# Turning the first softmax's weights by their layout (fp32 where strided, fp32r where contiguous) under a new order of all steps

## The chip, the cores and the metric

The kernel runs on one core of a Trainium2 chip. The metric is the device time of one execution in microseconds (us). A core has a matrix engine (TensorE, PE in the profile; PEld is its weight load), a vector engine (VectorE, DVE), a scalar engine (ScalarE, ACT), GpSimd (POOL) and a sync engine (SyncE, SP) that issues most of the DMA transfers. Each engine works through its own instructions in the order in which the program lists them and waits for the others through semaphores.

## The reference: what is computed

Two attentions through 32 "packing" queries per head, and then a feed-forward block with a gate from a convolution over the sequence:

```python
p_packed = sm_attn(p, k, v)                 # 8 batches x 8 heads: 32 queries over 576 keys, depth 64
out      = sm_attn(q, p_packed, p_packed)   # 576 queries over those 32
x        = out as [8, 576, 512]
h        = relu(x @ w_in)                   # w_in 512 x 1024
conv     = sum over k of conv_w[k] * h shifted by k - 1 along the sequence
y        = (h * sigmoid(conv)) @ w_out      # w_out 1024 x 512
```

`sm_attn` is scale, softmax (maximum taken off, exponential, division by the sum) and the product with the values. The two weight matrices and `conv_w` arrive as 64-bit floats and are rounded to fp32 on the chip.

## The kernel before, in words

The 64 heads form 16 groups `g` of four heads, so that four times 32 packing queries fill 128 partitions. For each group the kernel loads k, q and v; turns k and q so that the depth lies on the partitions (for the first four groups on TensorE, `half_transpose`, copied out by VectorE or ScalarE; later on VectorE); and runs `attention(g)`: scores of the packing queries with k (L752), maximum on VectorE, exponential on ScalarE (L890) into `a1_sb`, five turns of 128x128 on TensorE (L902), a copy to `a1T`, the product with v (L910), a copy `pb` scaled by the sums, one turn (L933) and its copy `ppT`, the scores with q (L752 again), the second softmax on VectorE, GpSimd and ScalarE, and its result split into a high and a low part in fp32r (`a2hi`, `a2lo`).

The five turns L902 are what the edit touches. They turn the exponentials, 128 queries by 576 keys, in pieces of 128 keys. For the first six groups (`g < APART`) v lies in SBUF with four neighbouring keys on one partition, so the first four turns each read every fourth column of `a1`; the fifth reads 128 neighbouring columns. For the other ten groups all five read neighbouring columns. Before, all five went through `a1_bits`, a view of the same memory as fp32r.

The rest is matrix work per batch `b`: `packed_weight` multiplies the packed values by w_in (L1107) and takes the low part by a matmul with minus the identity (L1135); `ffn1` makes 128 channels of the hidden layer from three fp32r products (L1196; L1170 for the first three channels' blocks of batch 0, which are cut in three steps); ScalarE and VectorE do relu, convolution and gate; `ffn2` multiplies by w_out (L1323 in plain fp32 for the first three tiles of 128 rows, L1376 in three fp32r products later, L1282 for the last tile). The weights of w_in and w_out are rounded by ScalarE (L463, L525: about a microsecond each), VectorE and GpSimd.

The order of everything is fixed ahead. The text `ORDER` names, two letters for a step, which of 268 streams (one per load, per attention, per block of channels and so on) goes next, and each engine gets its instructions in that order. Class `Flow` walks through it with a duration for every step, so as to decide one thing: where TensorE would wait in the first part, it puts matmuls on zeros, `warm` (L306), in the gap, as many as it thinks fit. `ON_DVE` and `ON_POOL` say which copies go to VectorE instead of ScalarE and which additions to GpSimd instead of VectorE. The search that finds `ORDER` is not in the kernel.

Of the kernel before, what the change touches and what calls it, by code (L numbers as in the profile page):

```python
# [18 lines left out]


ORDER = (
    "007f3603076y34023636036y340504050a040506050a70057001343a066z05056z350c34050e36340534050c3b0h0c053b0d0505340c7672"
    "3b0h7209360c050b050505080d713c36050j3b0b0c0c710c0c0j0c05050j0l3d3q053q0g770c0j3q0c0o0k0c3d3q3e0c0i0j3d0o0i0c0c73"
    "3d73740c3s740c3f3q3t3g3q3q0c0c3f780c3t3s3s0f3q3h3f3s0m0n3t3t0k3f793h3u3s0q3t3i3r0j3r0q3t3h0s0q3r3s0r3u3t0j3r3u3u"
    "0r370j0j3s0q0j0q3t0j0q3k3u0q0p3t3u3s0z3s0p753j3h0q3v0q7a753j3u3w0q3v3r3w3j0j3j400j3m0q5y370q3w3u3r0q3v0v405z3r3u"
    "3v603w3r5z5y3x3l7b603l0j3v0q3x3l373v3o403l0j0x0q3x400j0t3w3w3v0q0j0j0q0x5z5y0q123y0x3n0j3y3w0j3y3x3n3y3x60600x7c"
    "3n3y3z0x3z3z5y0j3n1441143p0q410x163x3z0u0q5z413x0y3p60605y0q7d143y3p190y15423z1d5z5z101e3y3j3l421142433z413p0w42"
    "43433z420x425y4444443l4342435z433n1445455y0x3j144515433n46605y441y0x456046464438440x4561451b46446046140x1b14465z"
    "0x471b3p45605y474846476113141g3p494847486149485z491761141b1b49485y1k484747614949486147496161616118141i0x4a141i62"
    "611i621c4b1b62621462621c1j140x630x380x4a1i62621b1b3862141i1b0x624a1i0x1j631a1z0x5z1n1r1b0x62141p626414141p636363"  # L30
    "141f1b0x634b63631b141i4b14631l141i631b4c1b1p4c641b4c1u631q4d1p4d4e1p1i644c1b1h4c4e4d4c1i1q1w1p644d651w1b1m1w644c"
    "4d4e1i251s4d1b4f1i1p4e4d4e4e646364641i641p211w644e654f4g1b1i4f1o1b1i1x4h4f4g641t6565644h1i1i1b4h651w4g4k1p4h4f23"
    "4g4k1i1p1x231w1p4f66651w6565234h4g4f4h4h1w1w4k1i4g6523651i234i6565661i4i1p4i1v284i4j66664j4g4i4j4i2a4l1p1w231w2a"
    "662a4m4i4n4j4j1p4j661p664m664j66664o1w4n4m666724672a244m1p6861391p671p4n1p23674n674o2k23674l2a6767674m4l4m204m4o"
    "4n4p4o232c2b4n66674p4n4q671w262a68391w222f232b4q394p4o4u4q274q4o2j4o234q2a692h2h694q2m1w684u1p4q4p6868681w1p4r4p"
    "4r1w2h68684u682d68682i4s4p2h4s294r4s2a691w6969692a4p692h234t4t2e68694t4s4r69694r2o1w4s4v4t6a6a2o2a692q2h1w6a2i4s"
    "4r6a2x2o4t4t4r6a6a4s4t236a2h2o6b2a236a6b1w2p236a6a69232h676a4w2o2a4x232t4w6b2h2a4w4y4v6c2p6b6b232l2g4w4w6b6b6b4y"
    "234w6b4x4w4z6b4x2v4z4y2z6b4y2a544v6c232h4x2o2v6d4y4z6c4x4x2v6c6a6c4z6c4z4x2h6c6c234y6c542v2h6c6d6c2h504y6b2a6d6e"
    "506d6d506d2h2a6d4z6d306d2r6e2w6c4z2n6d502w6d512v546f506e5051506e2o526e51516f2o516e6d6e53526e512h532o6e2a522a526e"
    "2y532v32556e2h2a2h2o51522a6f2a6f52322h322v556f6f6f2o536e5356522o6f6f6f2h53565757536f6g58562v6g2o562h6g6g6g575856"  # L40
    "576h576g6h566g562o6g586g6g58322o596g6h2o586h5755596h2s6i6g6h575a6h593258332v59585a5a6h6h59596i5a6h5b6j596h5a5a5b"
    "5c2o5c6i6i6j6i5b5a5d6i6i2o6i6h6i2h6i5d5c2u5b5e5c2v6i5f5b326j6j5b5d6j6j6j2o5e6f5d6j6j5c5d5d5c6i5b5e2o5d6j335f5c32"
    "2v2o6k6k5g2v5f5h5g2v5g6j326k6l5i6k5h6k5i5g5h2v326k6k6k5h5h5h316k5i5h5j6k6k5g6l325j5i6k5j325o325j5j5j5i6l6l6l6l6l"
    "6l322v6l6m5j5o6m6l6l5i5g325k5k6j6n6m6m5o6m2v6m6m5g5k5i6m6m5l5l6m2v5m322v6n2v5k6m5k322v5l6n325k6n5k5m6n6m5m5l6n6o"
    "5n5m5m6o326n5n6n5n5n6n6l6n6n2v5l5l5p325n5n6o5m5l326o6n6o5n6o6o5m6p6o326o5p6o5q5q5r5s5r5p6o5q6p6p6p6p6p5q5r5q5s6p"
    "5q5s6q6p5q6p6p5t6q5s6p5t5s5r6q6q5t6r5s6o5t6q5r6q6q5t5s5r5t6q6q5u6r6q5t5r5u6s5u6q5v5w6r6r5u5v5u5u6r5u6r5w5v6s5w6r"
    "5v5w5x6r6p5x5v6r5w5x6r6s5w6s5v6r6s6s6s5x5x5x5w5v6s5x6s6t6s6t6t6u6r6t6t6s6t6t6t6u6t6t6u6u6s6v6v6t6u6u6u6u6u6u6w6v"
    "6v6v6t6v6u6v6v6w6v6v6q6w6u6w6w6w6w6v6w6w6w6x6x6x6x6v6x6x6x6x6x6x6w7e7e6x7e6w7e7e7e7e6x7e7e7e"
)


# [171 lines left out]
def tile_packed_attention_conv_gate(  # L223
# [32 lines left out]
    ON_DVE = {"gh510", "hi0", "hi1", "hi12", "kT00", "kT05", "kT25", "kT30", "qT00", "relu34", "relu76", "tap00", "tap01", "tap21", "tap40", "tap41", "tap42", "tap44", "tap46", "tap53", "tap56", "tap57", "tap60", "tap61", "tap64", "tap65", "tap67", "tap70", "tap72", "tap73", "tap74", "tap75", "tap77", "x140", "x180", "x230", "x270", "x280", "x310", "x340", "x90"}
    ON_POOL = {"add00", "add01", "add10", "add41", "add51", "add61", "add70", "add71", "lo0", "lo10", "lo11", "lo7", "mul10", "mul12", "mul14", "mul2", "mul3", "mul4", "mul5", "mul6", "mul7", "mul9", "sub10", "sub11", "sub15", "sub2", "sub3", "sub4", "sub5", "sub7", "sub8", "sub9", "xl100", "xl110", "xl280", "xl30", "xl320", "xl330", "xl350", "xl50", "xl60", "xl70", "xl80"}
# [1208 lines left out]
```

## Time and profile before

| | |
|---|---|
| median of three runs | 392.18 us (392.03 to 392.35) |
| profiled execution: its own time | 392.02 us |
| its span, first to last instruction | 390.2 us |
| TensorE busy | 384.5 us, 99% of the span |
| VectorE, ScalarE, GpSimd busy | 332.1, 245.0, 73.8 us |
| matmuls on zeros (L306) | 16 |

The profiled execution's time is 1.8 us above its span. A busy interval of TensorE runs from an instruction's start to its modelled end, and neighbours overlap, so 99% busy doesn't mean that it never waited: waits that are shorter than an instruction's way through the array don't show. The distance from one start to the next start tells more.

### The profile page before, as it was taken

The page shows a single profiled execution, that of the slowest core. Times are in us where ns is not written, and L with a number is a line of the kernel's source. Part 1 is how long each engine was busy: PE and PEld are TensorE (multiplying, and loading weights), DVE is VectorE, ACT ScalarE, POOL GpSimd, SP SyncE. Part 2 cuts the span into 40 slices and gives each one's busy share as a digit, 9 for nine tenths or more (in the row PEclk, how much of TensorE's full clock was granted, in tenths as well). Part 3 has the DMA queues.
Part 4 walks back from the last instruction along what each step waited for, and adds up shares of the span by engine and source line. Part 5 has one row for each costly group of instructions (what it writes and reads, how often), then busy time and mean ns, then how long its engine had stood idle before and what let it go on. Part 6 is the DMA issues. An engine that isn't in the chain of part 4 may idle for free.

```text
span 390.2 us, 8180 instructions
## 1 busy us (share of the span) xinstructions
PE 384.5 (99%) x3299; PEld 308.0 (79%) x3299; DVE 332.1 (85%) x495; ACT 245.0 (63%) x403; POOL 73.8 (19%) x58
## 2 busy tenths in 40 slices
...
GB/s 278 372 391 275 198 311 146 203 141 192 93 185 146 179 18 182 198 139 152 116 103 135 29 87 89 0 29 55 29 2 54 55 28 29 27 0 29 81 54 56
DMA packets 157542, 47.62 MB, mean 122 GB/s; under 512 B 145460, under 2 KB 148788, under 8 KB 157504
## 3 DMA queue, kind: packets, MB, share of 16 engines
...
q8 instruction: 26, 0.43, 0.5%
q14 instruction: 12, 0.10, 0.1%
...
## 4 chain that ended last, share of the span: by engine, by line
PE 88%; ACT 4%; DMA 3%; DVE 2%; issue 1%; SPq 1%; ACTq 0%
PE fo L1376 42%; PE big L1196 24%; PE sm L1376 4%; PE big L1323 4%; PE big L752 4%; PE big L1107 3%; DMA k<-in_k_dram 2%; PE sm L910 2%; PE fo L1323 2%; PE big L902 1%; DMA hgt<-in_k_dram 1%; PE fo L1282 1%; PE sm L1282 1%; ACT tmp L463 1%; ACT tmp L525 1%
## 5 line engine op out<-in xcount | busy, mean ns | idle before, releaser
L1376 PE MATMUL fo<-wo_hi,xhi 128*128 128x512 f32 x232 | 93.3, 402 | 0.0
L1376 PE MATMUL fo<-wo_hi,xlo 128*128 128x512 f32 x232 | 90.8, 391 | 0.0
L1376 PE MATMUL fo<-wo_lo,xhi 128*128 128x512 f32 x232 | 90.5, 390 | 0.0
L1213 ACT ACTIVATE hbuf<-big 128x576 f32<-128x576 f32 x62 | 40.2, 656 | 45.7 <-PE big L1196 45.4
L1245 DVE SCALAR_TENSOR_TENSOR hgt<-hbuf,cw,hgt 128x576 f32<-128x576 f32 x64 | 53.4, 842 | 4.2 <-ACT hgt L1243 3.9
L1196 PE MATMUL big<-a2hi,ghi 128*128 128x288 f32 x244 | 55.3, 308 | 0.0
L1253 ACT ACTIVATE hgt<-hgt 128x576 f32<-128x576 f32 x64 | 43.3, 685 | 17.7 <-DVE hgt L1249 17.4
L1376 PEld LDWEIGHTS fo<-wo_hi,xhi 128*128 128x128 f32 x232 | 43.5, 188 | 11.3 <-issue 1.4
L1196 PE MATMUL big<-a2hi,glo 128*128 128x288 f32 x244 | 52.3, 295 | 0.0
L1196 PE MATMUL big<-a2lo,ghi 128*128 128x288 f32 x244 | 52.3, 295 | 0.0
L1249 DVE SCALAR_TENSOR_TENSOR hgt<-hbuf,cw,hgt 128x576 f32<-128x576 f32 x64 | 51.1, 810 | 0.5
L1376 PEld LDWEIGHTS fo<-wo_hi,xlo 128*128 128x128 f32 x232 | 43.6, 188 | 9.6
L1255 DVE SCALAR_TENSOR_TENSOR hgt<-hgt,hbuf 128x576 f32<-128x576 f32 x64 | 47.4, 752 | 3.4 <-ACT hgt L1253 2.8
L1376 PEld LDWEIGHTS fo<-wo_lo,xhi 128*128 128x128 f32 x232 | 43.6, 188 | 7.1
L1196 PEld LDWEIGHTS big<-a2hi,ghi 128*128 128x128 f32 x244 | 41.2, 189 | 6.2 <-issue 2.4
L352 POOL TENSOR_TENSOR xlo<-hgt,xhi 128x1024 fp32r<-128x1024 f32 x11 | 28.0, 2544 | 93.9 <-ACT xhi L359 38.2
L1391 ACT COPY o<-fo 128x512 f32<-128x512 f32 x30 | 17.5, 584 | 35.5 <-PE fo L1376 27.7
L1196 PEld LDWEIGHTS big<-a2lo,ghi 128*128 128x128 f32 x244 | 39.2, 189 | 0.0
L1196 PEld LDWEIGHTS big<-a2hi,glo 128*128 128x128 f32 x244 | 39.1, 188 | 0.0
L1243 ACT ACTIVATE hgt<-hbuf,cw 128x576 f32<-128x576 f32 x42 | 32.5, 778 | 2.9 <-DVE hbuf L1211 2.4
L352 POOL TENSOR_TENSOR s<-s,mx 128x576 f32<-128x576 f32 x10 | 14.3, 1433 | 100.6 <-DVE hgt L1249 58.4
L359 ACT CAST xhi<-hgt 128x1024 fp32r<-128x1024 f32 (+1 forms) x28 | 26.6, 952 | 9.2 <-PE fo L1376 4.0
...
## 6 DMA issues: line engine op xcount, KB each, us to landing
...
```

Of the source, the lines that this page charges most:

```text
L352: added = nc.gpsimd.tensor_tensor(**kw)
L359: nc.scalar.copy(out=out, in_=in_)
L1196: nc.tensor.matmul(out=t[:, hf, :SH], lhsT=w[:, gg, js], rhs=x[:, hf * SH : (hf + 1) * SH], start=n == 0, stop=n == (1 if b in F1F else 3) ...
L1213: nc.scalar.activation(out=inner, in_=t[:, :, :SH], func=AF.Relu, scale=0.5)
L1243: nc.scalar.activation(out=d, in_=h[:, 1 : S + 1], func=AF.Copy, scale=cw[:, NJ + j : NJ + j + 1])
L1245: nc.vector.scalar_tensor_tensor(out=d, in0=h[:, 0:S], scalar=cw[:, j : j + 1], in1=d, op0=ALU.mult, op1=ALU.add)
L1249: nc.vector.scalar_tensor_tensor(out=d, in0=h[:, 2 : S + 2], scalar=cw[:, 2 * NJ + j : 2 * NJ + j + 1], in1=d, op0=ALU.mult, op1=ALU.add)
L1253: nc.scalar.activation(out=d, in_=d, func=AF.Tanh)
L1255: nc.vector.scalar_tensor_tensor(out=d, in0=d, scalar=1.0, in1=h[:, 1 : S + 1], op0=ALU.add, op1=ALU.mult)
L1323: nc.tensor.matmul(out=t, lhsT=src[:, c, :], rhs=w32[c // 2][:, c % 2, :], start=c == 0, stop=c == NJ - 1)
L1376: nc.tensor.matmul(out=t, lhsT=x[:, c, :], rhs=w[:, c % 2, :], start=c + i == 0, stop=c == NJ - 1 and i == 2)
L1391: nc.scalar.copy(out=o, in_=t)
```

## The change

The turns of the strided pieces (four of five in groups 0 to 5) read `a1` as fp32 with the fp32 identity; the contiguous pieces (one of five there, all five from group 6 on) keep the fp32r view. The planner's durations are changed for these turns, for several loads and for the queue of transfers, and `ORDER`, `ON_DVE` and `ON_POOL` are those of a new search.

```diff
 ORDER = (
-    "007f3603076y34023636036y340504050a040506050a70057001343a066z05056z350c34050e36340534050c3b0h0c053b0d0505340c7672"
+    "3600367f07036y03366y340502010a053470050a0570050435063a04346z066z0534340e090c05050c36083b053b34053c0c76050d050c0h"
...
+    AHEAD = 2600
...
+            if step.issue:
+                at = max(at, self.data - self.AHEAD)
...
-    ON_POOL = {"add00", "add01", "add10", ...
+    ON_POOL = {"add01", "add10", ...
...
-        yield Step("SP", 3450, take=["kq"], sets=[(name, g)], parts=4, late=700, issue=830)
+        yield Step("SP", 3700 + 150 * (name == "q"), take=["kq"], sets=[(name, g)], parts=4, late=150, issue=810)
...
-        yield Step("PE", 544, take=["big", "a1T"], give=["a1"], cols=1280)
+        yield Step("PE", 525 if g < APART else 450, take=["big", "a1T"], give=["a1"], cols=1152 if g < APART else 640)
         t = big().rearrange("r f s -> r (f s)")
         for si in range(SV + 1):
-            if si == SV:
-                rows = a1_bits[:, S - 128 :]
-            elif g < APART:
-                rows = a1_bits[:, : 128 * SV].rearrange("c (r s) -> c s r", s=SV)[:, si, :]
+            if si < SV and g < APART:
+                rows = a1[:, : 128 * SV].rearrange("c (r s) -> c s r", s=SV)[:, si, :]
+                nc.tensor.transpose(out=t[:, si * 128 : (si + 1) * 128], in_=rows, identity=ident)
             else:
-                rows = a1_bits[:, 128 * si : 128 * si + 128]
-            nc.tensor.transpose(out=t[:, si * 128 : (si + 1) * 128].bitcast(F32R), in_=rows, identity=ident_r)
+                lo = min(128 * si, S - 128)
+                out = t[:, si * 128 : (si + 1) * 128].bitcast(F32R)
+                nc.tensor.transpose(out=out, in_=a1_bits[:, lo : lo + 128], identity=ident_r)
```

The added lines move the line numbers by three to four: L306 becomes L309, L463 L466, L728 L731, L752 L755, L910 L914, L933 L937, L1107 L1111, L1170 L1174, L1196 L1200; L902 becomes L902 (fp32) and L906 (fp32r).

How the order moves work, at three places. First TensorE in the first 20 us, from the product with v of group 0 to the turns of the keys of group 2 (`k`); `hgt_79` holds keys and queries of the first two groups, `stage` packing queries. Before:

```order
L910 MATMUL sm<-v_92,a1T 32x64 x20
L752 MATMUL big<-kT,pT 32x288 x8
L933 MATMUL sm<-ident,pb 128x128
L306 MATMUL idle<-zeros 128x512 x2
L539 MATMUL sm<-ident,cw_raw 128x24
L752 MATMUL big<-qT,ppT 32x288 x8
L728 MATMUL big<-ident,k 128x128 x5
L902 MATMUL big<-ident_r,a_bits 128x128 x5
L728 MATMUL big<-ident,k 128x128 x4
```

Of the change:

```order
L914 MATMUL sm<-v_92,a1T 32x64 x20
L755 MATMUL big<-kT,pT 32x288 x8
L937 MATMUL sm<-ident,pb 128x128
L309 MATMUL idle<-zeros 128x512 x5
L542 MATMUL sm<-ident,cw_raw 128x24
L755 MATMUL big<-qT,ppT 32x288 x8
L902 MATMUL big<-ident,a_sb 128x128 x4
L906 MATMUL big<-ident_r,a_bits 128x128
L731 MATMUL big<-ident,k 128x128 x9
L731 MATMUL big<-ident,hgt_79 128x128 x5
```

The turns of group 1's exponentials now stand ahead of the turns of the keys of group 2, and five matmuls on zeros instead of two fill the time up to the scores with q of group 0.

Second, ScalarE in the same stretch, from the copy `pb` of group 0 on (`tmp<-hgt_80` is the rounding of the first quarter of w_in, `ppT` what the scores with q wait for, `a_sb` the exponentials of group 1). Before:

```order
L923 ACTIVATE pb<-sm,rs 128x128
L359 COPY qT<-big 128x512
L545 ACTIVATE minus<-ident 128x128
L936 COPY ppT<-sm 128x128
L463 ACTIVATE tmp<-hgt_80 128x1024
L890 ACTIVATE a_sb,sm_266<-big,nm 128x576
```

Of the change:

```order
L927 ACTIVATE pb<-sm,rs 128x128
L466 ACTIVATE tmp<-hgt_80 128x1024
L940 COPY ppT<-sm 128x128
L894 ACTIVATE a_sb,sm_269<-big,nm 128x576
L528 ACTIVATE tmp<-hgt_80 128x1024
L362 COPY a1T<-big 128x640
```

The rounding of w_in now stands ahead of the copy `ppT`; it stood behind it.

Third, TensorE ahead of the first matmuls of `ffn1` (L1170, L1174): from the first product with w_in to them. Before:

```order
L1107 MATMUL big<-w_in_sb,ppT 32x256 x8
L902 MATMUL big<-ident_r,a_bits 128x128 x5
L306 MATMUL idle<-zeros 128x512 x2
L1135 MATMUL big<-ghi,minus 128x256 x2
L728 MATMUL big<-ident,k 128x128 x5
L306 MATMUL idle<-zeros 128x512 x2
L728 MATMUL big<-ident,q 128x128 x9
L728 MATMUL big<-ident,k 128x128 x4
L1170 MATMUL big<-a2hi,ghi 128x288 x2
```

Of the change:

```order
L1111 MATMUL big<-w_in_sb,ppT 32x256 x8
L309 MATMUL idle<-zeros 128x512
L731 MATMUL big<-ident,q 128x128 x5
L1139 MATMUL big<-ghi,minus 128x256 x2
L902 MATMUL big<-ident,a_sb 128x128 x4
L906 MATMUL big<-ident_r,a_bits 128x128
L309 MATMUL idle<-zeros 128x512
L731 MATMUL big<-ident,k 128x128 x5
L309 MATMUL idle<-zeros 128x512
L731 MATMUL big<-ident,k 128x128 x4
L731 MATMUL big<-ident,q 128x128 x4
L1174 MATMUL big<-a2hi,ghi 128x288 x2
```

Five of the nine turns of `q` (group 2) moved ahead of the turns of `k` (group 3); on SyncE their load moved ahead of that of `k` as well. Up to the first matmul of the main `ffn1` loop (L1196, L1200) both programs hold the same matmuls, but for 17 on zeros instead of 16 and the form of the turns. From there on, with the matmuls on zeros all behind it, the change lists the same work in another order, in 230 runs of one kind on TensorE where there were 245 (the whole program counted).

## Rows read from the trace of the kernel before

**Rows 1.** The page: its first line, and TensorE's row.

```profile
span 390.2 us, 8180 instructions
PE 384.5 (99%) x3299; PEld 308.0 (79%) x3299; DVE 332.1 (85%) x495; ACT 245.0 (63%) x403; POOL 73.8 (19%) x58
```

**Rows 2.** Windows: stretch, length, busy us and instructions by engine, clock, DMA share, GB/s.

```profile
4.00:45.40 41.40, 40.46 (x566) 28.90 (x565) 34.31 (x63) 35.12 (x65) 6.97 (x6) 1.00 0.99 318
91.50:385.50 294.00, 294.00 (x2359) 244.14 (x2358) 250.85 (x363) 164.87 (x272) 51.48 (x29) 1.00 0.38 82
```

**Rows 3.** Waits of TensorE, longest: us in total, times, longest.

```profile
PE big L728 <- DMA k<-in_k_dram: 0.5, 1, 0.5
```

**Rows 4.** Timeline of TensorE, 8 to 44 us: start, us, line, tiles, count.

```profile
8.93 1.31 PE L728 MATMUL big<-ident,hgt 128*128 128x128 f32 x10
10.04 0.85 PE L902 MATMUL big<-ident_r,a_bits 128*128 128x128 f32 x5
10.73 1.06 PE L728 MATMUL big<-ident,hgt 128*128 128x128 f32 x8
...
13.99 0.71 PE L752 MATMUL big<-qT,ppT 64*32 64x288 f32 x16
15.16 0.77 PE L728 MATMUL big<-ident,k 128*128 128x128 f32 x5 [0.46 <-DMA k<-in_k_dram]
15.68 0.83 PE L902 MATMUL big<-ident_r,a_bits 128*128 128x128 f32 x5
...
19.09 0.72 PE L752 MATMUL big<-kT,pT 64*32 64x288 f32 x16
...
27.25 0.54 PE L1170 MATMUL big<-a2hi,ghi 128*128 128x288 f32 x2
...
36.79 0.46 PE L306 MATMUL idle<-zeros 128*128 128x512 f32 x1
37.18 0.72 PE L752 MATMUL big<-qT,ppT 64*32 64x288 f32 x16
...
39.59 0.52 PE L1196 MATMUL big<-a2hi,ghi 128*128 128x288 f32 x2
39.95 0.43 PE L1196 MATMUL big<-a2lo,ghi 128*128 128x288 f32 x2
40.21 0.42 PE L1196 MATMUL big<-a2hi,glo 128*128 128x288 f32 x2
...
43.20 0.72 PE L752 MATMUL big<-qT,ppT 64*32 64x288 f32 x16 [0.17 <-ACT qT L359]
```

**Rows 5.** Timeline of ScalarE, 12 to 19 us.

```profile
13.50 0.27 ACT L936 COPY ppT<-sm 128x128 f32<-128x128 f32 x1
13.65 1.17 ACT L463 ACTIVATE tmp<-hgt 128x1024 f32<-128x1024 f32 x1
14.70 0.75 ACT L890 ACTIVATE a_sb<-big,nm 128x576 f32<-128x576 f32 x1
...
18.37 0.37 ACT L843 ACTIVATE pT<-big 128x256 f32<-128x256 f32 x1
```

**Rows 6.** L426, SyncE, window 5 to 6.2 us: first quarter of w_in, issue and landing.

```profile
L426 SPq DMA_DIRECT2D hgt<-in_moe_w_in_dram x1: 596/596/596, 5.6 to 5.6; - x1
...
DMA to landing us min/median/max: 8.0/8.0/8.0
```

**Rows 7.** L902's weight loads, groups 0 to 5: ns min/median/max.

```profile
L902 PEld LDWEIGHTS big<-ident_r,a_bits x30: 138/197/200, 10.0 to 76.8; 128*128 128x128 f32 x30
```

**Rows 8.** L902's weight loads, groups 6 to 15.

```profile
L902 PEld LDWEIGHTS big<-ident_r,a_bits x50: 138/140/143, 92.7 to 253.0; 128*128 128x128 f32 x50
```

**Rows 9.** L728's weight loads (fp32 turns of contiguous pieces), 7 to 27 us.

```profile
L728 PEld LDWEIGHTS big<-ident,hgt x27: 138/141/144, 8.9 to 18.8; 128*128 128x128 f32 x27
```

**Rows 10.** Timeline of TensorE around a turn of group 6 (contiguous).

```profile
92.91 0.54 PE L902 MATMUL big<-ident_r,a_bits 128*128 128x128 f32 x5
93.29 0.46 PE L1376 MATMUL fo<-wo_hi,xhi 128*128 128x512 f32 x1
```

More of the change, by code (lines that the diff above doesn't have):

```diff
@@ L27 @@
[L27 to L31, printed above, removed]
@@ L47 @@
-    "5v5w5x6r6p5x5v6r5w5x6r6s5w6s5v6r6s6s6s5x5x5x5w5v6s5x6s6t6s6t6t6u6r6t6t6s6t6t6t6u6t6t6u6u6s6v6v6t6u6u6u6u6u6u6w6v"
-    "6v6v6t6v6u6v6v6w6v6v6q6w6u6w6w6w6w6v6w6w6w6x6x6x6x6v6x6x6x6x6x6x6w7e7e6x7e6w7e7e7e7e6x7e7e7e"
+    "3600367f07036y03366y340502010a053470050a0570050435063a04346z066z0534340e090c05050c36083b053b34053c0c76050d050c0h"
+    "72050d0c0h720b053b360g3634050b050505710j713b0j0c0l050c0c050c0c053e0j3d3q0c0i0c3q0c3q0j773d3d3q0j0o3g0c0i740c0o73"
+    "0k0c3t0k0c3d740c733q3f3q3s783q0f0n0c0c3f3q3s3t0c3s3h3f3f3h3s3t0q0q3t793u3u3u0q0j3t3s3u3t0q0j0j0m3s3r0r3u0j3t3i3s"
@@ new lines @@
+    "0j3h0q3r0r0q3t3s3r0j3r0p3t3s750q0q0p3j0q3v3w3u7a3h750q3j3u373j3v3r0j3j3w3u0j0q403r0s3k3r3v3m373w0q0q0v3v3u3v3r40"
+    "0q0j3l3w3l3v5y5z5y60400z3x0t603v3w5z3o7b3x3l403w3y373x3l0j0x3y600q0j3w0q0j3x0q0j0q0x120j3n3y5z3z5z5y3n7c0x3z0x0u"
+    "60140j3l3x0x3n0j3x0y3y3n413p0x3z140q165y5y3p41143z41605z3x0q7d3z0q15423z413y3y3z423p0w0y3y3p0x154342431943424314"
+    "423j3j6044145y445y0x5z5z434244433n42444345465z4445443n451d46460x10173p3l4544601b4511450x145y61601b46451b18604746"
+    "5y46140x604761481g4761146113465z47490x6161481448471c4949483p49474849611e481k5z49474861611b611i145y1b4a611b490x14"
@@ new lines @@
+    "624b1i1i0x4a1i62141i62626262384b621c1b62140x38630x1b4a620x62380x1b1n1a1i14630x39620x1p141j14141j1b1i1b0x1463631b"
+    "1p1b1p14146363632k611r1u631f1p1b144b631i634c1q641l1i1p641h394c1b4c4d1q1m1i4d4c4d631b4c1w1p4e4c1p4e1i4d4d641s6364"
+    "1y1w64644e39651b1w1p64644e1w64644d1w4c4e1p4e4f25624d1o4g1b4e1i654f4h644g4h1b21234f1t4k4h1i4f1p4f1x1x234f1w4k4h65"
+    "4g651i664k4g656565654f1w234h6565661i1p4i1p234h651b1w661i4h4g4i1i1w4i1v1z1p64654j1i2c4j1p28661b4i664j231i4j244i66"
+    "4j2a4l1w231i4i4g4l661i242a661w4j2a4g4i66664m2b4j4l23662f674m674n4m4n4n4o1w2a681p67674m2a1w4m674n236767671p674m4m"
@@ new lines @@
+    "4o1w4n4o2b4n671w23674n264o1p201w1p4p224q2a4q68661p1w674p2e4p692h4q4o274o2h234u682j2d681w682368684p4q4p1p2h694p2a"
+    "684u4o236868684p4r4q4q4s2a4r6969234q1p2h2a6a69296a4s2h1w232m691w4u4t4t4r4t4s2i4s4s4r4t69696969694r4t1w2o4s4v2a2h"
+    "4t2o2l696a6a6a2q6a6a6a4t4s6a6a4r2i4r6b6b2h2o4v4v2p2a4w6a4w2p232t6a2r2x6b4w234x6b4y6b2o6b6b4w6b2a4w2g4w6b6b2a4y68"
+    "4y4w4z6c4y4x6b2h4x6c6c6c4x6b236c4x2a2o4y4z234x6c6c2h4y4z6c6c2a6d232o2h232v54544x6c4z2o6c2h4z6d2v506d506d236d6d6d"
+    "6d6d506d4z2o6e2v4y51546c4z2n502a2h6e6d30515052512o2w6f522a6e6e6e6e525250505152512v6e6e532v6e522v512a53326f2a2a2o"
@@ new lines @@
+    "51552a6e322o53536e2h56555653526d6e2s535656536f6f6f32562w566g6f2h2v6f2o6f566g6f6f576f57582h2o5757586g5857586g5959"
+    "6g6g6g6g6g59576g322z6f2h6h6g57552o6h5a2v5959596h6h6h6h586h592o5a5a5a5a2h6i585b6h6h6h5a582o5a5c326h2h6i2y2h2v6g5b"
+    "2h5c6i2h5c5d6i2u5c2o6h5b6i2o5b5c5d5d5b6i6i6i5d6i6i6j6i5c5e5f5b6j5e5d2o332v2o5c5d2v5d5b32336j6j6j6j6j6j6k2o6j6j5e"
+    "6k5g5h326j5g6i2v316k5g6l5g6k5i2v6k5h6k5g5f6k6k6k6k5f6l5g5g5h5h2v5i5i6k5h5i5j325i325j6l6l5j5h6l326l6l5j5j6l6l5i2v"
+    "326l5j6j6m6k5j325k6l5h5l6m6m2v6m5i2v6m6n5k5k5l32326m6m6m5k6m5l2v326n326m5k325m6m5l2v2v5m2v6n5k6l5m6n6n6n5k325n6n"
@@ L49 @@
+    "6o6n6m6n6n325l5n5n5o326n5p6o5m5l6o5m5o5n5n6o5n6o325o5m6o5p5m6o5p6o5q5n5q5l5r5r6o6o6p6p6o5s6p6p6o6p6p6q5r6p6p6p5q"
+    "5r6p5r5q5s5r5q5q5r5s6p5t5q6p5s5s6q5u5s6n6r5t5u5t6r6q5u5u6q5s6q6q6q6q6q5v5t5u5u5t5u5t5t6q5w5v5x6r5v6r6r6r6q5v6s6r"
+    "6r6r5v5x5v5w6r6s6s5x6s5w6q5x6r5w6s5x5v5x5w5w6s6s5x6s6s6s5w6t6t6t6t6t6s6t6t6t6u6u6t6t6s6u6u6u6u6t6u6t6r6v6v6u6u6u"
+    "6w6w6v6u6v6v6v6u6v6v6v6v6w6w6v6x6w6v6x6w6w6w6w6w6x6w6x6x6x6x6x6x6x7e7e7e7e7e7e6x6w6x7e7e7e7e"
 )
@@ L255, in tile_packed_attention_conv_gate @@
     PE_LO = 2
[L256 to L257 removed]
+    ON_DVE = {"a1T13", "a1T2", "hi0", "hi1", "hi10", "hi12", "kT00", "kT10", "qT05", "relu42", "relu45", "relu46", "relu51", "relu52", "relu70", "relu72", "relu74", "relu75", "relu76", "tap00", "tap01", "tap20", "tap22", "tap23", "tap32", "tap34", "tap36", "tap46", "tap47", "tap50", "tap51", "tap53", "tap61", "tap62", "tap63", "tap71", "tap72", "tap73", "tap75", "tap77", "x130", "x180", "x190", "x260", "x270", "x310", "x320", "x330", "x340"}
+    ON_POOL = {"add01", "add10", "add41", "add51", "add61", "add70", "add71", "lo0", "lo10", "lo11", "lo12", "lo7", "mul12", "mul14", "mul15", "mul2", "mul3", "mul4", "mul5", "mul6", "mul7", "mul8", "mul9", "sub10", "sub13", "sub2", "sub3", "sub4", "sub5", "sub6", "sub8", "xl120", "xl160", "xl30", "xl320", "xl50", "xl60", "xl70", "xl80", "xl90"}
     COLD = 7
@@ L268, in tile_packed_attention_conv_gate @@
     K1_FIRST = True
-    nc.alloc_sbuf_tensor("first", [128, S], F32)
+    nc.alloc_sbuf_tensor("a1_place", [128, S], F32)
     at = nc.sbuf_base - 4 * S
-    a1_sb, a1_bits = (
+    a1_views = [
         nc.alloc_sbuf_tensor_at(f"a1_{n}", [128, S], t, offset=at).ap() for n, t in (("sb", F32), ("bits", F32R))
-    )
+    ]
     cpool = ctx.enter_context(tc.tile_pool(name="consts", bufs=1))
@@ L422, in load_weight @@
         after = after + [("kh", 0)] * (i < 3)
-        yield Step("SP", (2700, 2700, 2750, 2900, 3000, 3600, 3600, 4200)[i], after=after, sets=[("wd", i)])
+        yield Step("SP", (2700, 2700, 2750, 2900, 3000, 3600, 3600, 4200)[i], after=after, sets=[("wd", i)], late=600 * (i in (5, 6)))
         if src.dtype != F32:
@@ L612, in load_v @@
             parts=2 if g < APART else 1 + HG,
-            late=(300 if g >= APART else 1500) * (g > 3),
+            late=(100 if g >= APART else 600) * (g > 3),
             issue=620 * (g >= APART),
```

24 lines of the change are left out of this document (3 added, 21 removed).

## The prediction

> **What bounds the kernel now.** I read the page first. TensorE is busy for 384.5 of 390.2 us [rows 1], so no other engine can give much. A busy share hides short waits, so the windows come next: from 91.5 us on TensorE is busy in all of 294.00 us and moves through its list at full clock, while the DMA engines have slack (0.38); from 4 to 45.4 us it is busy in 40.46 of 41.40 us and the DMA engines in 0.99 of the time [rows 2]. So behind the first 45 us the time is the sum of TensorE's own work, and only two things can change it: the price of an instruction, and how often TensorE changes the kind of work. Ahead of that, work waits for loads and for the chain of the first groups, and the gaps hold matmuls on zeros. The list of waits names one wait of TensorE behind the first microseconds that is worth a line, 0.5 us for the keys of group 2 [rows 3]; the timeline shows that wait and the zeros around it [rows 4]. What a new order can gain or lose lies in these first 40 us; the tail is the same work in both programs.
>
> **The turns.** A strided group takes 0.69 us from its first turn to the next work (10.04 to 10.73), a contiguous one 0.38 (92.91 to 93.29) [rows 4, 10], 0.076 a turn. So a strided turn takes (0.69 - 0.076) / 4 = 0.153. Its weight load takes 197 ns, a contiguous one 140 [rows 7, 8]: 57 ns more, and the turns stand 77 ns further apart, so the load sets the pace. In fp32 ten contiguous turns take 1.11 us (8.93 to 10.04) [rows 4], 0.111 each, with the same load of 141 ns [rows 9]: there something other than the load sets it, since the same load passes every 0.076 us in fp32r. No row shows a strided piece in fp32. Lower bound 0.111, if its load is hidden whole; upper bound 0.111 + 0.057 = 0.168, if the longer load adds whole. Between them I take the load's own pace as estimate, 0.076 + 0.057 = 0.133: above 0.111, so it would set the distance. A group then takes 4 x 0.133 + 0.076 = 0.61, 0.08 less. Only groups 4 and 5 lie in the packed stretch: -0.16 us, bounds -0.34 (0.111) and +0.12 (0.168). In groups 0 to 3 the turn lies between two waits and counts little.
>
> That the layout and not the type costs is what the rows show on this side: 197 against 140 ns in one type [rows 7, 8]. The Trainium skill (SBUF — State Buffer, section "Door 1: The DMA port swizzle") says why it may stay so: each access that moves to another 16-byte line of SBUF pays, and a step of four fp32 values is such a line, whatever view reads it. By that rule the turns would save nothing; by the rows' lower bound 0.34 us. It speaks against the change, and the trace agrees as far as it goes; it is a rival below.
>
> **The first 20 us.** The first quarter of w_in lands 8.0 us after its issue at 5.6, at 13.6 [rows 6]. Its rounding on ScalarE starts at 13.65 and holds the engine until the next instruction at 14.70, 1.05 us [rows 5]. Before, the copy `ppT` of group 0 (13.50) ran just ahead; now it stands behind. What is ahead in the DMA queue is unchanged, so the rounding can't start earlier, and `ppT` moves from 13.50 to about 14.70: 1.2 us. Behind it wait the scores with q (13.99 [rows 4], now about 15.19), and on ScalarE the exponential of group 1 (14.70, now 14.85). TensorE's list fits this: three more zeros stand in just that gap, and the turn of group 1 now follows the scores instead of the wait for the keys of group 2. That wait, from 13.99 to 15.16 with 0.46 idle [rows 4], goes, as the keys are there by then. Group 1's turn came 0.98 after the start of its exponential (15.68 - 14.70): now 15.83, when the scores with q have just ended. From 15.16 to 19.09, the scores of group 2 with k, TensorE needed 3.93 us, two zeros of about 0.39 each in it (36.79 to 37.18 shows one) [rows 4]. Without them 3.15, so 15.84 + 3.15 = 18.99: TensorE itself has caught up. But these scores also wait for the packing queries `pT`, which ScalarE copied 4.38 us after the scores with q of group 0 (18.37 - 13.99) [rows 4, 5], behind the second softmax's exponential, as now: 15.19 + 4.38 = 19.57 and a score 0.72 later (19.09 - 18.37), 20.29. One VectorE step of w_in's rounding has left that chain for a place ahead of it, about as long as the other such steps, so I take 19.6, some 0.5 us late, between 19.0 and 20.3.
>
> **Up to 43 us.** From there to the first `ffn1` product (27.25 [rows 4]) the program waits for the last two loads ahead of it, k of group 3 and q of group 2. They swap places in the queue with the same bytes, so the later one lands when it did. Behind it stood 13 turns (9 of q, 4 of k); now again 13 (9 of k, 4 of q) and one matmul on zeros between them. The zeros ahead fell from four to two. The lateness of 0.5 us is hidden by this wait: I put the start at 27.1, between 26.6 and 27.7. If that cover is not there, the cost is up to 1.2 us. From 27.25 to 39.59, the first product of the main loop, were 12.34 us, with one matmul on zeros (0.39, now gone) and one strided turn (0.08): 11.87 without new waits, first product at 39.0. ScalarE rounds w_in and copies for `ffn1` all this time and starts up to 0.5 us late; I take 39.5. At 43.20 the scores with q of group 3 waited 0.17 us for a copy on ScalarE [rows 4]; that copy stands at the same place behind the same rounding. So the head gives -0.1 us, bounds -1.2 and +1.2.
>
> **Changes of kind.** The first product behind an fp32 turn takes 0.36 us where its neighbours take 0.26 (39.59, 39.95, 40.21) [rows 4]: 0.10 for going from fp32 to fp32r. Counted in the two orders, TensorE goes from fp32 to fp32r work 28 times instead of 32, but enters the small tiles of scores and values once more. I take -0.2, between 0 and -0.4. The other moves of copies between ScalarE and VectorE and of additions between GpSimd and VectorE cost nothing while TensorE never waits for them, which it doesn't from 45 us on [rows 2]; uncovered, one such copy costs what it takes, 0.37 us for `pT` [rows 5].
>
> **Sum**, against the profiled execution's 392.02: -0.16 - 0.1 - 0.2 = -0.46, 391.56. The median of the runs, 392.18, is 0.16 above that execution: **391.7 us**. A difference under 0.2% (0.8 us) is about what a measurement of this kernel cannot tell from no change.
>
> **Rivals.** (1) *The head closes up.* The waits of the old list sit where steps came at other times than planned (the 1.17 us at 13.99, the zeros); the new list has them in other places. If `ffn1` starts at 26.6 and nothing waits up to the main loop, that begins at 38.4: -1.2, and with the turns at 0.111 and the changes of kind -0.34 and -0.2: 392.18 - 1.7 = 390.5. For it: every zero now lies ahead of the turns of group 3. Against: ScalarE. (2) *ScalarE's step is not absorbed.* The rounding ahead of `ppT` puts group 0's scores 1.2 us late, and from there the second softmax, `a2` and `ffn1`. It decides if the first `ffn1` product starts later than 27.7; with all of it passed on, 392.18 + 1.2 - 0.4 = 393.0: slower. (3) *The turns don't get cheaper.* The load keeps its 197 ns and the distance its 0.153 (the page's rule): 391.7 + 0.16 = 391.9, no change that can be told. (4) *A new wait behind 45 us*, for k, q, v or packing queries that are asked for later than before: 0.5 us a time, twice 392.7. The DMA engines' 0.38 there speaks against it.
>
> **How the numbers follow.** The forecast 0.30, (3) 0.14, (1) 0.36, (2) 0.13, (4) 0.07. Faster by over 0.2% (under 391.4): (1) and 0.04 of the forecast's low end, 0.40. Slower (over 393.0): half of (2), and what of (4) and of unknown waits in the head goes beyond its price, 0.16. The same: 0.44. The range leaves out the far end of (1) and of (2): 390.4 to 393.0; the likeliest case's own range is 391.2 to 392.2.
>
> **What would show it.** In the profile of the change: weight loads of the strided pieces, 140 or 197 ns, and 0.61 us from a strided group's first turn to the next work; the copy `ppT` of group 0 at about 14.7; the scores of group 2 with k at 19.0 to 20.3; the first `ffn1` product near 27.1; the first of the main loop near 39.5; no idle TensorE from 45 us on. I would be wrong if the main loop began before 38.7 or after 40.3, or if waits appeared behind it.

## The result and the profile after

The change is slower: 396.33 us, median of 5 runs (395.57 to 396.83), against 392.35 (392.03 to 393.07) for the kernel before on the same chip; ratio 1.0097, 95% interval 1.0081 to 1.0114. The profiled execution took 396.39 us, its span is 394.6 us, 4.4 more than before. Among the runs further below, one execution of 423.4 us (`kT` on VectorE) and one of 757.3 us (kernel before) stand far out: they are counted in the medians of the table, which they hardly move, and not in the ratios.

The page of the change, its first line and TensorE's row:

```profile
span 394.6 us, 8174 instructions
PE 385.0 (98%) x3300; PEld 308.2 (78%) x3300; DVE 339.4 (86%) x507; ACT 240.9 (61%) x394; POOL 65.6 (17%) x55
```

TensorE does as much as before [rows 1]; the time is waiting. The windows of the change say where (columns as in [rows 2]):

```profile
4.00:45.40 41.40, 39.82 (x558) 28.73 (x565) 33.76 (x62) 35.09 (x66) 4.95 (x4) 1.00 1.00 313
91.50:140.00 48.50, 45.25 (x528) 35.20 (x530) 43.65 (x70) 28.81 (x51) 14.91 (x9) 1.00 0.81 155
91.50:385.50 294.00, 290.75 (x2329) 240.89 (x2328) 259.03 (x376) 160.19 (x261) 44.74 (x27) 1.00 0.39 83
```

All 3.25 idle microseconds behind 91.5 us lie ahead of 140. Before, TensorE was busy in all of that stretch [rows 2]. The three waits in TensorE's timeline:

```profile
118.89 0.53 PE L1200 MATMUL big<-a2lo,ghi 128*128 128x288 f32 x2 [1.55 <-DVE a2lo L352]
121.70 0.72 PE L755 MATMUL big<-qT,ppT 64*32 64x288 f32 x16 [0.43 <-DVE qT L691]
137.55 0.72 PE L755 MATMUL big<-kT,pT 64*32 64x288 f32 x16 [1.27 <-DVE kT L691]
```

All three wait for VectorE. Its timeline shows that VectorE waits as well, for loads:

```profile
103.39 0.70 DVE L873 STREAM_TRANSPOSE pT<-stage 128x512 f32<-128x512 f32 x1
...
116.81 1.38 DVE L691 STREAM_TRANSPOSE kT<-k 128x1152 f32<-128x1152 f32 x1 [3.25 <-DMA k<-in_k_dram]
118.11 0.72 DVE L352 TENSOR_TENSOR a2lo<-a2t,a2hi 128x576 fp32r<-128x576 f32 x1
120.27 1.38 DVE L691 STREAM_TRANSPOSE qT<-q 128x1152 f32<-128x1152 f32 x1 [0.24 <-DMA q<-in_q_dram]
...
136.02 1.38 DVE L691 STREAM_TRANSPOSE kT<-k 128x1152 f32<-128x1152 f32 x1 [1.19 <-DMA k<-in_k_dram]
```

The first wait names `a2lo`, which needs no load: it only stands behind the turning of k in VectorE's list. The loads are late because they were asked for late, as SyncE's timeline shows (start, length, issues):

```profile
95.62 10.64 SPq L867 DMA_DIRECT2D stage<-in_p_dram  x8
106.31 3.34 SPq L629 DMA_DIRECT2D v<-in_v_dram  x4
109.75 0.60 SPq L632 DMA_DIRECT2D v<-in_v_dram  x1
110.45 0.55 SPq L1400 DMA_DIRECT2D out_dram<-o  x1
111.05 3.20 SPq L671 DMA_DIRECT2D k<-in_k_dram  x4
114.35 3.25 SPq L671 DMA_DIRECT2D q<-in_q_dram  x4
```

Eight issues of packing queries take 10.64 us. SyncE's list of waits has the reason, and a narrower window of its timeline (99 to 106.3 us) the start of the last four:

```profile
SPq L867 <- DVE sm L966: 5.5, 1, 5.5
```

```profile
104.12 2.14 SPq L867 DMA_DIRECT2D stage<-in_p_dram  x4
```

The eight issues are two loads, for groups 8 to 11 and for 12 to 15, and both go to the same columns of `stage`. The second can't be issued until VectorE has turned the first, at 103.39 to 104.09. (The list of waits names `sm`, the short instruction on VectorE that starts at 104.01, as the turn ends.) In the order before, the two loads stood far apart on SyncE, and the wait never showed:

```profile
80.52 2.31 SPq L863 DMA_DIRECT2D stage<-in_p_dram  x4
...
145.93 2.22 SPq L863 DMA_DIRECT2D stage<-in_p_dram  x4
```

SyncE issues in order, so v, a store, k and q all stood behind the blocked load. The planner has a token for most buffers but none for these columns: for the last two lots `queries` takes nothing (`take=["o"] * (i < 2)`).

In the first 45 us the change is late as well. ScalarE:

```profile
13.85 1.12 ACT L466 ACTIVATE tmp<-hgt 128x1024 f32<-128x1024 f32 x1 [0.94 <-DMA hgt<-in_moe_w_in_dram]
14.87 0.26 ACT L940 COPY ppT<-sm 128x128 f32<-128x128 f32 x1
15.01 0.76 ACT L894 ACTIVATE a_sb<-big,nm 128x576 f32<-128x576 f32 x1
```

TensorE's scores with q of group 0 stand at 15.35, the scores of group 2 with k at 19.94, the first `ffn1` product at 28.08 and the first of the main loop at 40.70 (before 13.99, 19.09, 27.25 and 39.59 [rows 4]).

### The profile page after: what moved, and what is told of

Read it like the earlier page. It is cut to its first block, busy times and chain, and to the rows that moved or that the text cites. A ratio compares the mean times of both kernels' runs of the same rounds, so it can differ in the third digit from the quotient of the medians.

```text
span 394.6 us, 8174 instructions
## 1 busy us (share of the span) xinstructions
PE 385.0 (98%) x3300; PEld 308.2 (78%) x3300; DVE 339.4 (86%) x507; ACT 240.9 (61%) x394; POOL 65.6 (17%) x55
## 4 chain that ended last, share of the span: by engine, by line
PE 82%; DVE 8%; DMA 5%; SPq 2%; ACT 2%; issue 1%; DVEq 0%; ACTq 0%
PE fo L1380 37%; PE big L1200 22%; PE sm L1380 4%; PE big L1327 4%; PE big L755 3%; PE big L1111 3%; DMA hgt<-in_q_dram 3%; SPq L671 2%; PE fo L1327 2%; PE sm L914 2%; DMA k<-in_k_dram 1%; DMA q<-in_q_dram 1%; PE idle L320 1%; PE fo L1286 1%; PE sm L1286 1%
## 5 line engine op out<-in xcount | busy, mean ns | idle before, releaser
L1249 DVE SCALAR_TENSOR_TENSOR hgt<-hbuf,cw,hgt 128x576 f32<-128x576 f32 x64 | 51.9, 817 | 4.1 <-ACT hgt L1247 3.5
L1200 PE MATMUL big<-a2hi,ghi 128*128 128x288 f32 x244 | 54.9, 306 | 0.0
L1200 PE MATMUL big<-a2lo,ghi 128*128 128x288 f32 x244 | 52.4, 296 | 1.6 <-DVE a2lo L352 1.6
L1217 ACT ACTIVATE hbuf<-big 128x576 f32<-128x576 f32 x54 | 35.3, 665 | 29.4 <-PE big L1200 29.1
L1200 PE MATMUL big<-a2hi,glo 128*128 128x288 f32 x244 | 52.4, 296 | 0.0
L1253 DVE SCALAR_TENSOR_TENSOR hgt<-hbuf,cw,hgt 128x576 f32<-128x576 f32 x64 | 51.2, 810 | 0.4
L1259 DVE SCALAR_TENSOR_TENSOR hgt<-hgt,hbuf 128x576 f32<-128x576 f32 x64 | 48.3, 763 | 3.0 <-ACT hgt L1257 2.9
L1200 PEld LDWEIGHTS big<-a2hi,ghi 128*128 128x128 f32 x244 | 41.3, 189 | 5.8 <-issue 1.2
L1200 PEld LDWEIGHTS big<-a2lo,ghi 128*128 128x128 f32 x244 | 39.1, 188 | 1.8 <-DVE a2lo L352 1.8
L1247 ACT ACTIVATE hgt<-hbuf,cw 128x576 f32<-128x576 f32 x43 | 33.3, 784 | 10.1 <-DVE hbuf L1215 9.5
L1200 PEld LDWEIGHTS big<-a2hi,glo 128*128 128x128 f32 x244 | 39.2, 189 | 0.0
L355 POOL TENSOR_TENSOR xlo<-hgt,xhi 128x1024 fp32r<-128x1024 f32 x9 | 22.1, 2451 | 89.8 <-DVE xhi L360 48.3
L352 DVE TENSOR_TENSOR xlo<-hgt,xhi 128x1024 fp32r<-128x1024 f32 (+1 forms) x28 | 30.4, 1098 | 5.5 <-ACT xhi L362 5.1
L355 POOL TENSOR_TENSOR s<-s,sm 128x576 f32<-128x576 f32 x11 | 13.5, 1227 | 80.5 <-DVE s L352 35.3
```

Source lines behind the costliest of these rows:

```text
L352: nc.vector.tensor_tensor(**kw)
L355: added = nc.gpsimd.tensor_tensor(**kw)
L1200: nc.tensor.matmul(out=t[:, hf, :SH], lhsT=w[:, gg, js], rhs=x[:, hf * SH : (hf + 1) * SH], start=n == 0, stop=n == (1 if b in F1F else 3) ...
L1217: nc.scalar.activation(out=inner, in_=t[:, :, :SH], func=AF.Relu, scale=0.5)
L1247: nc.scalar.activation(out=d, in_=h[:, 1 : S + 1], func=AF.Copy, scale=cw[:, NJ + j : NJ + j + 1])
L1249: nc.vector.scalar_tensor_tensor(out=d, in0=h[:, 0:S], scalar=cw[:, j : j + 1], in1=d, op0=ALU.mult, op1=ALU.add)
```

## The experiments

| kernel | median us (runs) | before, same chip | ratio, 95% interval |
|---|---|---|---|
| own columns for the last packing queries | 392.71 (12) | 392.71 | 1.0008 (0.9982 to 1.0034) |
| old order, new turns | 392.69 (12) | 392.71 | 0.9989 (0.9971 to 1.0006) |
| `ppT` first | 396.18 (6) | 392.71 | 1.0078 (1.0050 to 1.0107) |
| own columns, `ppT` first | 392.98 (12) | 392.71 | 1.0001 (0.9984 to 1.0018) |
| old order, load moved forward | 397.73 (4) | 392.51 | 1.0136 (1.0122 to 1.0151) |
| own columns, `kT` on VectorE | 392.98 (11) | 392.51 | 1.0011 (1.0001 to 1.0020) |
| load moved back | 392.98 (12) | 392.51 | 1.0006 (0.9992 to 1.0020) |
| own columns, old turns | 392.60 (11) | 392.51 | 1.0005 (0.9995 to 1.0015) |
| own columns, `ppT` and turns of k first | 393.11 (12) | 392.89 | 1.0014 (0.9995 to 1.0034) |
| old order, load forward, own columns | 392.71 (11) | 392.89 | 0.9990 (0.9980 to 1.0001) |
| old order, load forward, place for a store | 395.72 (8) | 392.89 | 1.0065 (1.0042 to 1.0088) |

### Own columns

```diff
-            raw = stage[:, : 4 * HG * 32].rearrange("n (g d) -> n g d", d=32)
+            raw = stage[:, 512 * (i - 2) : 512 * (i - 1)].rearrange("n (g d) -> n g d", d=32)
```

> The packing queries of the last four groups are loaded to columns of `stage` of their own, so that their load need not wait until VectorE has turned those of the four groups before; order and everything else are those of the change. Theory (SyncE's queue is blocked by the shared columns): the 5.5 us wait of SyncE goes, the load of k behind it begins at 104 to 105.5 us instead of 111.05, and the three waits of TensorE at 116.9, 121.7 and 137.6 us (1.85, 0.72 and 1.56 us by the distance of starts) go with it: 396.4 - 4.1 = 392.3 us, at least 3 us faster than the change. Rival (k, q and v are late because the transfers themselves are slow there, or because VectorE's list is late): SyncE's wait goes, the waits of TensorE stay, and the time is within 0.8 us of the change.

SyncE, the windows and TensorE in this kernel (all engines' lists are those of the change):

```profile
95.23 5.17 SPq L867 DMA_DIRECT2D stage<-in_p_dram  x8
...
104.02 4.11 SPq L671 DMA_DIRECT2D k<-in_k_dram  x4
```

```profile
91.50:140.00 48.50, 48.50 (x551) 37.98 (x550) 48.13 (x78) 33.03 (x58) 15.46 (x10) 1.00 0.91 172
```

```profile
45.77 0.50 PE L1139 MATMUL big<-ghi,minus 128*128 128x256 f32 x2
...
116.90 0.43 PE L1200 MATMUL big<-a2lo,ghi 128*128 128x288 f32 x2
...
119.12 0.72 PE L755 MATMUL big<-qT,ppT 64*32 64x288 f32 x16
...
133.62 0.71 PE L755 MATMUL big<-kT,pT 64*32 64x288 f32 x16
```

TensorE's waits are gone. The same instructions stood at 46.08, 118.89, 121.70 and 137.55 us in the change: a lead of 0.31 us grows to 1.99, 2.58 and 3.93, that is by 3.62 us over the three places. The median falls by as much (396.33 to 392.71, on two chips; `ppT` first, which keeps the waits, had 396.18 on this one). The theory holds: as far as these runs can tell (interval 0.9982 to 1.0034), the whole loss against the kernel before is the blocked queue. My 4.1 had taken off too little, 0.13 us each, for the distance that the same starts have without a wait (0.26, 0.36 and 0.36 us with own columns).

### Old order, new turns; and own columns, old turns

The edit of the five turns shown in the change's diff, in the kernel before; and the reverse of it beside own columns.

> The kernel before, with its order and its durations, and only the form of the turns changed (fp32 for the strided pieces of groups 0 to 5). Theory (a strided turn takes 0.12 to 0.125 us in fp32 instead of 0.153): 0.05 us less in a group, 0.1 to 0.2 us less over groups 4 and 5, which lie in the packed stretch, and little in groups 0 to 3: 0.1 to 0.4 us faster than before, not to be told from it by the time alone. Rival (reading every fourth column costs the same in either type): 0.69 us from a strided group's first turn to the next work, as before, and no difference. Second rival (the longer weight load, 196 to 220 ns, makes fp32 dearer): slower by 0.1 to 0.4 us.

> Own columns as before, and the strided turns again in fp32r, as in the kernel before: the price of the form in the new order. Theory (0.12 to 0.125 us a turn in fp32, 0.153 in fp32r; 0.04 to 0.05 us in a group): groups 4 and 5 together give back 0.1 us and the head little, so within 0.3 us of own columns alone, a strided group at 0.68 to 0.70 us from its first turn to the next work instead of 0.64. Rival (fp32 saves 0.3 us and more by the fewer changes of kind around the turns): 0.3 to 0.6 us slower than own columns alone.

Group 0 takes 0.54 us from its first turn to the next work in the old order with fp32 turns (9.79 to 10.33) instead of 0.69 [rows 4], more than expected. Groups 4 and 5, which stand in the packed stretch, tell less of a gain. Group 4 before, and in the old order with fp32 turns:

```profile
57.02 1.88 PE L1323 MATMUL fo<-w,hgt 128*128 128x512 f32 x4
58.34 1.11 PE L902 MATMUL big<-ident_r,a_bits 128*128 128x128 f32 x5
59.29 0.50 PE L1196 MATMUL big<-a2hi,ghi 128*128 128x288 f32 x2
```

```profile
56.67 1.88 PE L1323 MATMUL fo<-w,hgt 128*128 128x512 f32 x4
58.39 0.63 PE L898 MATMUL big<-ident,a_sb 128*128 128x128 f32 x4
58.78 0.30 PE L902 MATMUL big<-ident_r,a_bits 128*128 128x128 f32 x1
58.92 0.48 PE L1196 MATMUL big<-a2hi,ghi 128*128 128x288 f32 x2
```

From the first turn to the next work it is 0.53 us instead of 0.95. But the first turn starts later by nearly as much, counted from the product ahead of it (1.72 us behind its start instead of 1.32), so product and group together take 2.25 us instead of 2.27. Group 5 counted so takes 1.39 instead of 1.41; in the new order, fp32 against fp32r, it is 2.24 against 2.26 and 0.80 against 0.83. Both groups together save 0.04 to 0.05 us. One thing that works against the change is that the contiguous fp32r turn behind the fp32 ones takes 0.14 us (58.78 to 58.92), where it takes 0.08 behind fp32r ones (61.38 to 61.46 with own columns and old turns).

The times can't show so little. From the first product of the main loop to the end, which holds groups 4 and 5, the old order took 350.3 us (389.6 - 39.27) with fp32 turns and 350.6 with fp32r; the new one 350.4 (390.6 - 40.17) with fp32 and 350.3 (390.8 - 40.53) with fp32r: the signs differ.

### `ppT` first, alone and with more

Two neighbouring steps of the order are swapped, the rounding `3b` and the copy `05`:

```diff
-...36083b053b34...
+...3608053b3b34...
```

> The change with two neighbouring steps of the order swapped: on ScalarE the copy `ppT` of group 0 again ahead of the rounding of the first quarter of w_in. Zeros on TensorE follow the planner: two instead of five ahead of the scores with q. Theory (the lateness of ScalarE's step is passed on to the main loop): `ppT` at 13.6 instead of 14.87 us, the scores with q of group 0 at 14.0 to 14.2, the first product of ffn1 near 27.2 and of the main loop near 39.8: 0.7 to 1.1 us faster than the change, 395.3 to 395.7. The waits behind 90 us stay. Rival (the last loads, or VectorE's list, set the start of ffn1): first product of ffn1 still at 28.0, time within 0.3 us of the change.

> Own columns and `ppT` first together. If both theories hold the gains add: 396.4 - 4.1 - 0.9 = 391.4 us, 0.7 to 1 us faster than the kernel before, with no wait of TensorE behind 45 us. If one of them is wrong, its part is missing: 392.3 without the head's, 395.5 without that of the queue. If the waits move to another place once the queue is free, 392.5 or more.

ScalarE did what was asked, TensorE gained nothing. ScalarE, then TensorE, with `ppT` first:

```profile
13.82 0.27 ACT L940 COPY ppT<-sm 128x128 f32<-128x128 f32 x1 [0.51 <-PE sm L937]
13.98 1.16 ACT L466 ACTIVATE tmp<-hgt 128x1024 f32<-128x1024 f32 x1
15.04 0.73 ACT L894 ACTIVATE a_sb<-big,nm 128x576 f32<-128x576 f32 x1
```

```profile
14.34 0.72 PE L755 MATMUL big<-qT,ppT 64*32 64x288 f32 x16
14.98 0.96 PE L309 MATMUL idle<-zeros 128*128 128x512 f32 x3
15.92 0.75 PE L902 MATMUL big<-ident,a_sb 128*128 128x128 f32 x4
...
20.01 0.72 PE L755 MATMUL big<-kT,pT 64*32 64x288 f32 x16
```

The scores with q came 1.01 us earlier, but the exponential of group 1 starts at 15.0 either way, behind the rounding, and TensorE multiplies zeros until it is out. The main loop began at 40.75, the time stayed (396.18 us). With own columns as well, 391.4 us was expected and 392.98 came. So the place of `ppT` costs nothing that shows, and this explanation fails. Two further tries at the head, each beside own columns:

```diff
-    ON_DVE = {... "kT10", "qT05", ...
+    ON_DVE = {... "kT10", "kT25", "qT05", ...
```

> Own columns as before, and the copy `kT` of the second half of group 2's keys on VectorE, as in the kernel before, and not on ScalarE. Theory (ScalarE bounds the head from 13.8 us on, and the extra copy puts 0.6 us on its chain up to the packing queries' copy `pT` and ffn1): `pT` 0.4 to 0.6 us earlier behind the exponential of group 1, the first product of ffn1 and of the main loop 0.3 to 0.6 us earlier than with own columns alone (27.35 and 40.17 us there), time 0.3 to 0.6 us lower. Rival (the loads or the rounding of the third quarter of w_in set the main loop's start): within 0.2 us of own columns alone.

The main loop began at 41.04, later and not earlier; `pT`, at 19.51, waited 0.27 us for TensorE. This explanation fails too.

In the last, with `ppT` first, the turns of group 1's exponentials (`0c`) and the first turns of k (`0h`) are swapped:

```diff
-...0c0h72...
+...0h0c72...
```

> Own columns and `ppT` first, and besides the first five turns of the keys of group 2 ahead of the turns of group 1's exponentials on TensorE again, as in the kernel before. Theory (in the new order TensorE has only zeros to do from the end of the scores with q of group 0, at 15.0 us, until the exponential of group 1 is out at 15.9, and does the turns of k behind it, so that bringing `ppT` forward alone gave nothing): the five turns fill 15.1 to 15.7, the scores of group 2 with k come some 0.5 us earlier than 19.61, and the first product of the main loop 0.4 to 0.8 us earlier than 40.47: 39.7 to 40.1, time 392.2 to 392.6. Rival (the head waits for w_in's quarters or for ScalarE, whatever TensorE does): main loop within 0.2 us of 40.47.

The turns of k stood at 15.16, the scores of group 2 with k at 19.48, the main loop at 40.32, where 39.7 to 40.1 was expected. This fails as well.

### Load moved back

The second load stands behind those of k and q that followed it, in shared columns. Its step `39` comes 30 steps later in `ORDER`, behind that of q of group 7 (`1f`):

```diff
-    39
...
     1f
+    39
```

> The change with one step of the order moved: the load of the packing queries of the last four groups behind the loads of k and q that it stood ahead of, in the same shared columns. Theory (what costs is that the blocked load stands ahead of k and q in SyncE's queue): no wait of TensorE over 0.3 us behind 45 us, time that of own columns (392.0 to 393.0 us), 3.2 to 3.9 us less than the change. Rival (the shared columns or the extra transfers themselves cost): 395 us or more.

The time is that of own columns: the shared columns cost nothing where the load stands behind k and q, so it is its place on SyncE, with them, that makes the loss. One expectation missed: v, now behind the load, held TensorE (timeline):

```profile
121.93 0.32 PE L914 MATMUL sm<-v,a1T 128*32 128x64 f32 x8 [1.03 <-DMA v<-in_v_dram]
```

### The same block in the old order

Here the load moves forward in the kernel before (`39` from step 703 to 474 of 1502, and its condition in the planner from the scores of group 7 to those of group 3); then with own columns; then in shared columns with a place of its own for the copy of one output tile.

> The kernel before, with the load of the packing queries of the last four groups moved forward in SyncE's list, from 145.9 us to the first place behind the turning of the four groups before it (in SyncE's list between the loads of q at 92.8 and of v at 101.1 us), in the same shared columns of `stage`. SyncE is then blocked until VectorE has turned the first lot (102.5 to 103.2 us), so v is asked for some 4 us later and k (106.3) and q (110.7) some 2 to 3 us. Theory (a blocked queue costs lateness less slack): in this order k is asked for by 109.4, lands near 113 and is turned at 116.7, q lands near 116.8 and is turned at 119.0, so slack of 2 to 4 us covers it and the time is that of the kernel before, at most 0.5 us more, while SyncE shows the wait of some 5 to 7 us. Rival (any block of the queue is passed on whole): 2 to 4 us slower.

Slower by 5.2 us, more than either side expected. TensorE's list of waits, its timeline around the wait, and windows behind it:

```profile
PE fo L1376 <- ACT o L1391: 3.3, 1, 3.3
```

```profile
112.60 0.80 PE L1376 MATMUL fo<-wo_hi,xhi 128*128 128x512 f32 x1 [3.26 <-ACT o L1391]
113.19 0.63 PE L1376 MATMUL fo<-wo_lo,xhi 128*128 128x512 f32 x1
113.62 0.63 PE L1376 MATMUL fo<-wo_hi,xlo 128*128 128x512 f32 x1
...
118.53 0.39 PE L1376 MATMUL fo<-wo_hi,xlo 128*128 128x512 f32 x1
118.75 0.39 PE L1376 MATMUL fo<-wo_hi,xhi 128*128 128x512 f32 x1
```

```profile
109.20:112.60 3.40, 0.14 (x9) 0.01 (x1) 3.38 (x6) 0.64 (x2) 1.16 (x1) 0.83 0.97 196
112.60:117.90 5.30, 5.30 (x13) 4.15 (x14) 2.93 (x5) 3.44 (x6) 1.43 (x1) 0.50 1.06 197
```

I had looked at k, q and v behind the block, and not at the store between them. It left at 108.2 instead of 103.9 us, so its buffer `o` came free late, ScalarE's copy of TensorE's results into `o` waited for it (4.24 us, for the DMA), and TensorE for that copy. Behind 3.26 us without work TensorE ran at a granted clock of 0.50, 1.2 GHz: products 0.43 us apart instead of 0.23. How much of the loss is the low clock differs from run to run: the other three executions took 397.4 to 398.7 us at a mean clock of 0.994 to 0.996, this one 397.9 at 0.990.

> The kernel before with the load of the last packing queries moved forward as in the experiment on the old order, but to columns of its own. Theory (what cost 5.2 us there is SyncE's wait for the shared columns alone): no wait of SyncE for VectorE, no wait of TensorE for the copy to `o`, and the time of the kernel before, 392.0 to 393.0 us. Rival (the transfer itself in that place, or its four issues ahead of v, cost): 394 us or more.

As expected, 392.71: moving the load costs nothing without the shared columns.

```diff
-        o = wk.tile([128, DM], F32, name="o", tag="o")
+        o = stage[:, 1024:1536] if m == 4 else wk.tile([128, DM], F32, name="o", tag="o")
```

> The kernel before with the load moved forward in shared columns, so that SyncE is blocked as in that experiment, but the copy of the fifth output tile goes to a place of its own (unused columns of `stage`) and need not wait until an earlier tile has left its buffer. Theory (the loads have slack, and TensorE waited 3.3 us at 109.3 because a store of the output stood behind the blocked load and so kept the buffer that ScalarE's copy, and through it TensorE, waited for; the time at 1.2 GHz behind it is a consequence): SyncE's wait of some 7 us stays, the wait and the low clock go, 392.3 to 393.3 us. Rival (late k and q would have held TensorE in any case): 394.5 us or more, with waits for kT or qT at 118 to 125 us.

SyncE's wait stayed (7.1 us), the wait at 109 and the low clock went, but a wait that had been hidden behind it came out:

```profile
124.12 0.72 PE L752 MATMUL big<-qT,ppT 64*32 64x288 f32 x16 [1.83 <-DVE qT L688]
```

Still 2.8 us slower (single executions from 393.8 to 397.4): the rival was right that the late q holds TensorE in any case. I had reckoned with a q that is asked for 2 to 3 us late; in this profile it was asked for at 115.63 us, 4.9 later than before (110.73), and VectorE stood idle for 2.21 us ahead of turning it.

## Why the prediction was wrong, point by point

**What bounds the kernel.** The step that failed is here: "behind the first 45 us the time is the sum of TensorE's own work, and only two things can change it". A third could: loads that are asked for later. That was rival (4), which I gave 0.07 and put at 0.5 us a time because the DMA engines' share is 0.38. The mechanism was among the rivals, its price was not: three waits, 3.62 us. The DMA share says that transfers have room, not that they are asked for. I compared the orders on TensorE and ScalarE in the first 45 us and did not read SyncE's list behind that, where the two loads of packing queries had become one row of eight issues. Both signs that I had named for being wrong came: the main loop began at 40.70, and waits appeared behind it.

**The turns.** Predicted: the distance of strided turns falls from 0.153 to 0.133, the load setting it. The load did not shorten, it grew, as this row of the change's weight loads shows (before 197 [rows 7]):

```profile
L902 PEld LDWEIGHTS big<-ident,a_sb x24: 196/209/220, 10.0 to 72.2; 128*128 128x128 f32 x24
```

The turns still stand closer, about 0.12 us against 0.14 where single ones follow each other (in group 4 of the old order, starts at 58.50, 58.62 and 58.74 in fp32, at 58.92, 59.06 and 59.20 in fp32r). So the load doesn't set the distance; that the estimate came near was luck. (Its ground, 57 ns of load for 77 ns of distance, was no fit either.) The sum of -0.16 did not come. It took the 0.69 us of group 0 for groups 4 and 5, which stood 0.95 in the kernel before, and the distance from the first turn to the next work doesn't tell what a group costs: counted with the product ahead, both groups saved 0.04 to 0.05 us. The rule of the Trainium skill (SBUF — State Buffer, section "Door 1: The DMA port swizzle"), that each new 16-byte line costs, was the ground of rival (3). The trace agrees for the load, 209 ns against 141 for neighbouring columns in the same type [rows 9], and not for the distance of the turns, which got shorter in a type of the same width. The result for the time was that of rival (3).

**The first 20 us.** `ppT` at 14.87 (14.7), the exponential at 15.01 (14.85), the scores with k at 19.94 (19.6, between 19.0 and 20.3): held.

**Up to 43 us.** "The lateness of 0.5 us is hidden by this wait" failed: 0.85 us late at 19.94, still 0.83 at 28.08 and 1.11 at 40.70. A single execution is a rough measure here, since the same head stood at 19.12, 27.35 and 40.17 in the profile of own columns. The main loop began at 39.27 to 40.06 us in five profiles of the old order's head and at 40.17 to 40.70 in four of the new one. Counted from the start of ScalarE's first rounding of w_in (13.65 before, 13.85 in the change) the two heads part clearly: 25.94 to 26.02 us in four of the five (26.61 in the fifth) against 26.74 to 26.85 in the four, some 0.8 late. Rival (2) gave the right sign, but for its cause the runs speak against it, since `ppT` first brought nothing that shows. Nor did the copy `kT` or the turns of k. The cause of this lateness is not settled, nor what it costs in the end: the medians with own columns, in either form of the turns, lie 0.0 and 0.1 us above those of before. What is shown is that together with all the rest of the change it comes to less than the measurement tells.

**Changes of kind.** Predicted -0.2 beside the turns' -0.16. The stretch from the main loop to the end took 350.3 to 350.8 us in four profiles of the new order with own columns and fp32 turns, and 350.6 and 350.4 in two of the old order with fp32r turns (before; load forward with own columns): no gain is seen, and the term was mis-sized.

**In sum**, without the blocked queue the change is a change of nothing that can be told, near the -0.46 us of the forecast, but not for its reasons, as none of the three terms came as sized; the blocked queue adds 3.6 us.
